# Banded attention and a gated block on one core: P.V products grouped by tile shape, low parts of w_out summed on TensorE, zero matmuls ahead of early transposes, new due times

## The chip, the cores and the metric

The kernel runs on one core of a Trainium2 chip. The metric is device time in microseconds: 289.54 us before the change, the median of three runs (288.92 to 289.74). A profile of one further execution goes with it. Engines are named as in the profile: PE is TensorE's matmuls, PEld its weight loads, DVE is VectorE, ACT ScalarE, POOL GpSimd, SP the queue that issues DMAs.

## The reference

Attention over 4 batch elements, 8 heads, 768 positions, head width 64; a row sees the first 8 positions and the last 96, with a linear bias by head. Its output is the input of a gated block: a causal depthwise convolution of 5 taps gives the gate, `x @ w_val` the value, and the gated value goes through `w_out`.

```python
scores = scale * np.matmul(q, k.transpose(0, 1, 3, 2))
keep = is_global | is_local
scores = np.where(keep, scores + bias[None], -1000000000.0)
a = np.exp(scores - np.max(scores, axis=-1, keepdims=True))
a = a / (np.sum(a, axis=-1, keepdims=True) + 1e-09)
attn = np.matmul(a, v)                       # then to (B, S, 512) as x
for k in range(5):
    gate_pre += conv_w[k][None, None, :] * xp[:, k:k + S, :]
gate = 1.0 / (1.0 + np.exp(-gate_pre))
out = gate * (x @ w_val) @ w_out
```

## The kernel before, in words

**Tiling.** A group is one batch element, one half of its positions (3 blocks of 128 rows) and one pair of heads: 32 groups, 96 steps (a step is one block of one group, numbered `s`). A step has a window of 168 columns per head (128 for the first block of a batch element, whose steps are the first of each first-half group). Scores come on TensorE in 64x64 tiles (`scores`, L451), VectorE adds the bias and takes the row minimum (L459), ScalarE takes the exponential with its row sum (L469), GpSimd or VectorE adds the small constant (L476) and normalizes (`p`, L484), VectorE inverts (L479). TensorE transposes the probabilities into a PSUM tile `pt` (L492; three transposes a step, two in a first block), of which there are two banks; ScalarE or VectorE copies it out (`a`).

**P.V.** `pv` (L499) runs for a pair of groups at a time, the last two groups alone. For each block it first takes the 128-row products (L510: 128 rows of `a` against `vs` or `v0`, on a 128x64 tile), then, unless the block is a first one, two rounds of 64-row products (L513, on 64x64 tiles), and goes on to the next block. An fp32 product shows as two instructions. From the fifth group on (index 4) the scores of a later group follow P.V directly. The result `x` stays in PSUM, in two buffers.

**Gated block.** A phase is one half of a batch element, four groups. `x` is split into a high and a low fp32r part (`xh`, `xl`), VectorE convolves it (L613), ScalarE takes the sigmoid, TensorE makes `val` with three fp32r products per chunk (L659), VectorE gates it, the gated value is split again, and TensorE makes the output tile `o` (L679), which needs all four chunks of `w_out`.

**Weights.** They come as 64-bit floats and are rebuilt from integer halves, chunk by chunk (four of `w_val`, four of `w_out`): one ScalarE step (L331), four VectorE steps (L339 to L348), then a high part `wvh` or `woh`. The low part is the remainder. For `w_val` TensorE adds it up in PSUM (`w_sum`, L373: the identity times the whole, minus one times the high part, plus one times the rest) and ScalarE or VectorE copies it out. For `w_out` two elementwise steps on GpSimd or VectorE do it (`w_rest`, `w_low`, L364 and L369).

**What sets the order.** `Plan` (L57) lists all operations with a due time ("urgency"), a cost per engine and what they wait for, and writes one order for all engines: at each point the free engine takes the most urgent ready operation. `plan.ring` keeps the use of a set of buffers in a fixed sequence. The constants at the top (L17 to L29) are due times and costs. Eight zero matmuls at the start and three behind the first scores (L254) are in the plan too. Each engine works its instructions off in the order written.

Of the kernel before, what the change touches and what calls it, by code (L numbers as in the profile page):

```python
# [15 lines left out]
AX = mybir.AxisListType  # L16
WARM = 8  # L17
S_B, PT_B, X_B = 2, 2, 2
U_D1, RAW_B = -1.42, 4
FILL_N, FILL_TO, U_F = 1, 1, -3.23  # L20
W_AT = (-0.65, 1.85, 4.45, 6.35, 17.51, 17.64, 22.06, 22.56)
SPARE = {'vector': 1.0, 'gpsimd': -0.11, 'scalar': -0.06}
XH_B, GATE_B, P_B, T_B, A_B, V_B, W_B, WT_B = 7, 2, 5, 8, 13, 6, 2, 1
U_XE, U_XH, U_CV, CV_STEP = 0.93, -0.23, 2.87, 0.59
U_AM, U_EX, U_RC, U_PT, U_EV, U_MOE = 0.47, 0.84, -0.36, -0.38, 3.52, 18.1
# [3 lines left out]
U_SG, U_GM, GM_STEP, U_GH, U_GL, U_O, VAL_T, O_T, U_OE = 1.99, -0.17, 2.17, 2.27, -3.94, 6.16, 7.45, 4.99, 1.44  # L29
PSUM = bass.MemoryType.PSUM  # L30

B, H, S, D = 4, 8, 768, 64
P = 128
NP = H // 2
NB = S // P
DM = H * D
# [20 lines left out]
class Plan:  # L57
# [3 lines left out]
    DMA_LAT, DMA_RATE = 1.6, 330e3  # L61

    def __init__(self):
        self.ops, self.at, self.rings, self.then = [], {}, {}, {}

    def add(self, key, urgency, engines, fn, deps=(), nbytes=0):

        assert key not in self.at, key
        self.at[key] = len(self.ops)
        self.ops.append((urgency, engines, fn, list(deps), nbytes))  # L70

    def follow(self, key, other):

# [12 lines left out]
    def order(self, start):  # L86
# [16 lines left out]
        while avail:  # L103
            cands = []
            for i in avail:
                t = {e: max(free[e], ready(i, e)) for e in ops[i][1]}
                e = min(t, key=lambda x: t[x] + ops[i][1][x] + SPARE.get(x, 0.0))
                cands.append((t[e], i, e))
            first = min(cands)
            _, i, e = min(  # L110
                ((ops[i][0], i, e) for t, i, e in cands if e == first[2] and t <= first[0] + 1e-9)
            )
            while i is not None:
                t = max(free[e], ready(i, e))
# [12 lines left out]
                i = self.then.get(i)  # L127
# [5 lines left out]
def attention_moe(ctx, tc, qT, kT, kg, vs, vo, v0, v, counts_in, wv, cw, wo, out):  # L133
# [199 lines left out]
    def f64_op(e, raw, n, nm, k):  # L333
# [10 lines left out]
        elif k == 3:  # L344
            ve.tensor_scalar(out=yi, in0=T[nm, "h"][:, :n], scalar1=-0x800000, scalar2=None, op0=ALU.bitwise_and)
        else:
            r = tile_of((nm, "r"), [P, DM], F32 if nm[1] >= NC else F32R, "wr", WT_B)[:, :n]
# [13 lines left out]
        h, c = (wvh, i) if i < NC else (woh, i - NC)  # L361
        copy(e, h[:, c], T[("w", i), "h"].bitcast(F32))

    def w_rest(e, i):  # L364
        h, c = (wvh, i) if i < NC else (woh, i - NC)
        x = T[("w", i), "h"].bitcast(F32)
        engine(e).tensor_sub(x, x, h[:, c])

    def w_low(e, i):  # L369
        l, c = (wvl, i) if i < NC else (wol, i - NC)  # L370
        engine(e).tensor_add(l[:, c], T[("w", i), "h"].bitcast(F32), T[("w", i), "r"])

    def w_sum(i):  # L373

        ps = tile_of(("wsum", i), [P, DM], F32, "moe", 2, psum)
        nc.tensor.matmul(ps, ident, T[("w", i), "h"].bitcast(F32), start=True, stop=False)
        nc.tensor.matmul(ps, units[:, 1], wvh[:, i], start=False, stop=False)
        nc.tensor.matmul(ps, units[:, 0], T[("w", i), "r"], start=False, stop=True)

    plan.ring("moe", 2, ("WARM",), [("WARM",)] + [("F", s) for s in range(3 * FILL_TO)])  # L380
    for i in range(2 * NC):
# [13 lines left out]
                     lambda e, i=i, k=k: f64_op(e, T["w", i], DM, ("w", i), k), deps)  # L395
        plan.add(("WH", i), u + 0.5, {ACT: 0.52, DVE: 0.335}, lambda e, i=i: w_high(e, i), [("W2", i), ("W3", i)])
        if i < NC:
            key = ("WS", i)
            plan.add(key, u + 0.6, {PE: 1.6}, lambda e, i=i: w_sum(i),
                     [("WH", i), ("W4", i), ("UNITS",)] + plan.ring("moe", 2, key, [("WP", i)]))  # L400
            plan.add(("WP", i), u + 0.7, {ACT: 0.47, DVE: 0.65},
                     lambda e, i=i: copy(e, wvl[:, i], T["wsum", i]), [("WS", i)])
            continue
# [82 lines left out]
    def transpose(s):  # L486

        pt = tile_of(("pt", s), [P, 4 * P], F32, "pt", PT_B, psum)
        pr = T["p", s].rearrange("p two n -> p (two n)")
        starts = (0, SW) if width(s) == P else (0, 2 * SW - P, SH)  # L490
        for i, c in enumerate(starts):
            nc.tensor.transpose(pt[:, i * P : (i + 1) * P], pr[:, c : c + P], ident)  # L492
# [4 lines left out]
        copy(e, a[:, :n], pt[:, :n])  # L497

    def pv(gs):  # L499
        for k in range(HB):  # L500
            w = width(HB * gs[0] + k)
            runs = [(g, j, head_at(groups[g][2], j), T["a", HB * g + k]) for g in gs for j in range(2)]
            c0 = HIST + k * P

            def rows(i):
                return slice(i * D, (i + 1) * D)

            for g, j, i, a in runs:
                v = T["v0", g][:, j] if w == P else T["vs", g][:, k, j]
                nc.tensor.matmul(T["x", g][rows(i), c0 : c0 + P], v, a[:, j * P : (j + 1) * P], start=True, stop=w == P)  # L510
            for h in range(2 if w == SW else 0):
                for g, j, i, a in runs:
                    nc.tensor.matmul(T["x", g][rows(i), c0 + h * QH : c0 + (h + 1) * QH], T["vo", g][rows(j), k, h],  # L513
                                     a[rows(j), 2 * P + h * QH : 2 * P + (h + 1) * QH], start=False, stop=h == 1)

    SCORES, SWITCH = 0.285, 0.1

# [2 lines left out]

    def pv_cost(gs):
        steps = HB if groups[gs[0]][1] else HB - 1
        return (0.64 if len(gs) == 2 else 0.43) * steps + 0.21 * len(gs) * (HB - steps)

    def s_deps(g):
        deps = [("Lrk", g), ("Lrq", g)]
# [33 lines left out]
    for g, (b, hf, p) in enumerate(groups):  # L560
        for k in range(HB):
# [23 lines left out]
            key = ("PT", s)  # L585
            plan.add(key, s + U_PT, {PE: 0.42 if full else 0.31}, lambda e, s=s: transpose(s),
                     [("NM", s, 0), ("NM", s, 1), ("IOTA",)] + plan.ring("pt", PT_B, key, [("EV", s)]))
# [369 lines left out]
```

## Time and profile before

| what | us |
|---|---|
| median of three runs | 289.54 |
| the profiled execution | 290.27 |
| its span, first to last instruction | 288.5 |
| PE busy | 267.1 (93%) |
| PEld busy | 216.6 (75%) |
| DVE busy | 202.4 (70%) |
| ACT busy | 213.7 (74%) |
| POOL busy | 142.4 (49%) |
| mean granted TensorE clock | 0.969 of full |

Busy time is the union of an engine's instructions, so overlapping matmuls count once. In a timeline a row is a run of like instructions: start, time to the end of the last, and their number; time in brackets is idle time of the engine before the row, with what ended it. The distance between the starts of two neighbouring rows is what the first took from the queue.

### The profile page before, as it was taken

Reading aid. Unit: us, or ns where it says so; the run is one execution under the profiler, and the core shown is the slowest. Engines: PE = TensorE matmul, PEld = TensorE weight load, DVE = VectorE, ACT = ScalarE, POOL = GpSimd, SP = SyncE. Lnnn points to the kernel's source line nnn. Section 1 sums busy time; section 2 is a strip of 40 time slices with the busy share of each in tenths; the row PEclk is TensorE's granted clock in tenths of the full one; section 3 lists DMA queues with packets and bytes.
Section 4 is the critical chain, followed back from the end, with each engine's and each line's share of the span. In section 5 each row is a group of like instructions: output and inputs, shape, how many; then the busy total and the mean of one; then the engine's idle time right before and its main releaser. Section 6 shows DMA issues by size and latency. Waiting matters only on the chain.

```text
span 288.5 us, 8778 instructions
## 1 busy us (share of the span) xinstructions
PE 267.1 (93%) x3084; PEld 216.6 (75%) x3084; DVE 202.4 (70%) x780; ACT 213.7 (74%) x658; POOL 142.4 (49%) x341
## 2 busy tenths in 40 slices
PE   7499785898999999999999999999999999999991
PEld 3266563585788978897789887987889888877981
DVE  3877999679496949596859775893959594946200
ACT  3779959666689969895979779985799589745220
POOL 5967467838332862476226812580348342720320
PEclk9779998599999999999999999999999999999999
DMA  6989965040464606350637063423641021001012
GB/s 161 313 254 316 314 184 181 28 128 3 139 210 124 189 36 186 101 180 9 210 138 222 28 182 136 131 64 99 214 157 55 3 76 39 0 2 73 36 42 80
DMA packets 25683, 36.38 MB, mean 126 GB/s; under 512 B 3104, under 2 KB 21536, under 8 KB 25632
## 3 DMA queue, kind: packets, MB, share of 16 engines
q1 hardware_dynamic: 25632, 35.75, 39.2%
q8 instruction: 26, 0.43, 0.6%
q14 instruction: 25, 0.20, 0.2%
HBM read 29.45 MB, written 6.29 MB: 124 GB/s over the span
## 4 chain that ended last, share of the span: by engine, by line
PE 72%; DVE 9%; POOL 6%; ACT 4%; issue 3%; DMA 3%; SPq 0%; POOLq 0%; ACTq 0%
PE val L659 21%; PE o L679 20%; PE x L510 9%; PE pt L492 9%; PE s L451 7%; PE x L513 6%; POOL p L484 3%; DVE gate L613 3%; DVE t L459 2%; POOL bias L318 2%; DMA vo<-in_vo 1%; DMA counts_i<-in_counts 1%; ACT p L469 1%; ACT gate L615 1%; POOL sm L476 1%
## 5 line engine op out<-in xcount | busy, mean ns | idle before, releaser
L469 ACT ACTIVATE p<-t,mins 128x168 f32<-128x168 f32 (+1 forms) x192 | 82.9, 437 | 10.2 <-DVE mins L459 8.6
L484 POOL TENSOR_SCALAR p<-p,rs 128x168 f32<-128x168 f32 (+1 forms) x179 | 75.2, 434 | 30.4 <-DVE rs L479 23.4
L613 DVE SCALAR_TENSOR_TENSOR gate<-x,cwt,gate 128x384 f32<-128x384 f32 x128 | 77.7, 612 | 1.3 <-ACT gate L615 0.5
L459 DVE CUSTOM_DVE_ANT_0 t<-s,bias 128x168 f32<-128x168 f32 (+1 forms) x192 | 56.7, 316 | 3.5 <-PE s L451 2.9
L492 PE MATMUL pt<-ident,p 128*128 128x128 f32 x272 | 51.3, 291 | 8.2 <-POOL p L484 6.1
L476 POOL TENSOR_SCALAR sm<-sm 128x2 f32<-128x2 f32 x94 | 19.2, 204 | 74.4 <-ACT p L469 66.0
L492 PEld LDWEIGHTS pt<-ident,p 128*128 128x128 f32 x272 | 34.4, 144 | 22.3 <-POOL p L484 14.5
L659 PE MATMUL val<-xh,wvh 128*128 128x384 f32 x128 | 47.1, 368 | 0.4 <-DVE g L666 0.4
L672 POOL TENSOR_TENSOR gl<-g,gh 128x384 fp32r<-128x384 f32 x32 | 32.5, 1014 | 25.6 <-ACT gh L155 24.5
L659 PE MATMUL val<-xl,wvh 128*128 128x384 f32 x128 | 43.2, 338 | 1.3 <-DVE xl L605 1.3
L659 PE MATMUL val<-xh,wvl 128*128 128x384 f32 x128 | 43.1, 337 | 0.0
L679 PE MATMUL o<-woh,gh 128*128 128x512 f32 x96 | 42.0, 437 | 1.0 <-DVE rs L479 1.0
L155 ACT COPY a<-pt 128x384 f32<-128x384 f32 (+1 forms) x84 | 38.7, 461 | 5.0 <-PE pt L492 4.7
L451 PE MATMUL s<-rk,rq 64*64 64x64 f32 (+3 forms) x1088 | 34.9, 265 | 3.9 <-DVE ('w', 0)_h L342 3.0
L469 ACT ACTIVATION_READ_ACCUMULATOR p<-t,mins 128x1 f32 x192 | 38.5, 200 | 0.0
L679 PE MATMUL o<-woh,gl 128*128 128x512 f32 x96 | 38.0, 396 | 0.0
L679 PE MATMUL o<-wol,gh 128*128 128x512 f32 x96 | 37.9, 395 | 0.0
L605 DVE TENSOR_TENSOR xl<-x,xh 128x384 fp32r<-128x384 f32 x32 | 17.5, 553 | 28.5 <-ACT gate L615 14.7
L451 PEld LDWEIGHTS s<-rk,rq 64*64 64x64 f32 x1088 | 30.9, 135 | 8.7 <-issue 5.8
L155 ACT CAST xh<-x 128x384 fp32r<-128x384 f32 x32 | 15.1, 479 | 23.1 <-PE x L513 18.3
L479 DVE RECIPROCAL rs<-sm 128x2 f32<-128x2 f32 x96 | 15.1, 159 | 21.1 <-POOL sm L476 20.1
L510 PE MATMUL x<-a,vs 128*64 128x128 f32 x320 | 28.0, 295 | 0.0
(149 smaller groups left out, 402.5 us busy)
## 6 DMA issues: line engine op xcount, KB each, us to landing
rq<-in_qT SPq DMA_DIRECT2D x32, 192.0 KB, 3.5
out<-ob SPq DMA_DIRECT2D x24, 256.0 KB, 2.0
rk<-in_kT SPq DMA_DIRECT2D x16, 252.0 KB, 3.4
rk<-in_kT SPq DMA_DIRECT2D x16, 200.0 KB, 3.1
vs<-in_vs SPq DMA_DIRECT2D x16, 192.0 KB, 3.3
vo<-in_vo SPq DMA_DIRECT2D x16, 192.0 KB, 3.3
w<-in_wv SPq DMA_DIRECT2D x4, 512.0 KB, 4.4
vs<-in_vs SPq DMA_DIRECT2D x16, 128.0 KB, 3.3
```

The source lines that it names most:

```text
L155: nc.scalar.copy(dst, src)
L451: nc.tensor.matmul(s[rows, u : u + w], T["rq", g][r, k * P + half * QH : k * P + (half + 1) * QH], T["rk", g][r, c : c + w], start=True, s ...
L459: nc.vector.tensor_tensor_reduce(out=t[:, :n], in0=T["s", s // HB, s % HB, j][:, :n], in1=bias[:, h, :P] if n == P else bias[:, h, P:], op ...
L469: nc.scalar.activation(T["p", s][:, j, :n], T["t", s, j][:, :n], AF.Exp, bias=mins[:, s, j : j + 1], scale=-1.0, accum_out=T["sm", s][:, j ...
L476: engine(e).tensor_scalar(out=sm, in0=sm, scalar1=1e-9, scalar2=1.0, op0=ALU.add, op1=ALU.mult)
L484: engine(e).tensor_scalar(out=pr, in0=pr, scalar1=rs, scalar2=1.0, op0=ALU.mult, op1=ALU.mult)
L492: nc.tensor.transpose(pt[:, i * P : (i + 1) * P], pr[:, c : c + P], ident)
L510: nc.tensor.matmul(T["x", g][rows(i), c0 : c0 + P], v, a[:, j * P : (j + 1) * P], start=True, stop=w == P)
L613: nc.vector.scalar_tensor_tensor(out=gt, in0=src, scalar=w, in1=gt, op0=ALU.mult, op1=ALU.add)
L659: nc.tensor.matmul(T["val", ph, m], (wvh, wvh, wvl)[r][:, c, m * P : (m + 1) * P], (T["xh", g], T["xl", g], T["xh", g])[r], start=(c == 0 ...
L672: engine(e).tensor_sub(tile_of(("gl", ph, m), [P, HT], F32R, "gl", 5), T["g", ph, m], T["gh", ph, m])
L679: nc.tensor.matmul(T["o", ph, k], (T["gh", ph, c], T["gl", ph, c], T["gh", ph, c])[r][:, cols], (woh, woh, wol)[r][:, c], start=(c == 0 an ...
```

## The change

`pv` takes all 128-row products of a batch first, over its three blocks, and then all 64-row products. `w_rest` and `w_low` go; `w_out` chunks use `w_sum` as `w_val` does, in the PSUM ring of the transposes, behind the transposes of steps 17, 18, 23 and 24. The plan counts, for each transpose that it puts before its time 80, how many zero matmuls fit into the time for which it sees TensorE idle (at most 12), and `transpose` issues them into its own PSUM tile first. All due times get new values.

```diff
-U_D1, RAW_B = -1.42, 4
-FILL_N, FILL_TO, U_F = 1, 1, -3.23
-W_AT = (-0.65, 1.85, 4.45, 6.35, 17.51, 17.64, 22.06, 22.56)
-SPARE = {'vector': 1.0, 'gpsimd': -0.11, 'scalar': -0.06}
+U_D1, RAW_B = -4.08, 4
+FILL_UNTIL = 80.0
+FILL_N, FILL_TO, U_F = 1, 1, -4.6
+W_AT = (-1.16, 2.02, 7.13, 10.68, 17.77, 19.65, 21.85, 24.91)
+WS_AT = (17, 18, 23, 24)
+SPARE = {'vector': 0.99, 'gpsimd': 0.02, 'scalar': -0.16}
...
-U_L, U_LV, U_WL, U_S, U_HI, U_NM = -13.8, -2.88, -2.19, -1.88, -1.27, 0.16
-U_PH = (-4.57, -2.14, -0.94, 0.0, 0.0, -0.17, 0.0, 3.57)
+U_L, U_LV, U_WL, U_S, U_HI, U_NM = -19.46, -1.44, -0.21, -1.87, -2.32, -2.58
+U_PH = (-5.31, -2.3, -1.09, -0.3, -0.58, -0.33, -3.9, 2.9)
...
+                if ops[i][5] is not None and t < FILL_UNTIL:
+                    bank = max([end[at[d]] + self.LAT[where[at[d]]] for d in ops[i][5]], default=0.0)
+                    self.fill[i] = max(0, min(12, int((t - max(free[e], bank) - 0.15) / 0.215)))
...
     def w_sum(i):
-        ps = tile_of(("wsum", i), [P, DM], F32, "moe", 2, psum)
+        tag, bufs = ("moe", 2) if i < NC else ("pt", PT_B)
+        high = wvh[:, i] if i < NC else woh[:, i - NC]
+        ps = tile_of(("wsum", i), [P, DM], F32, tag, bufs, psum)
         nc.tensor.matmul(ps, ident, T[("w", i), "h"].bitcast(F32), start=True, stop=False)
-        nc.tensor.matmul(ps, units[:, 1], wvh[:, i], start=False, stop=False)
+        nc.tensor.matmul(ps, units[:, 1], high, start=False, stop=False)
         nc.tensor.matmul(ps, units[:, 0], T[("w", i), "r"], start=False, stop=True)
...
-        plan.add(("WS", i), u + 0.6, {POOL: 1.33, DVE: 0.62}, lambda e, i=i: w_rest(e, i), [("WH", i), ("W3", i)])
-        plan.add(("WP", i), u + 0.7, {POOL: 1.33, DVE: 0.62}, lambda e, i=i: w_low(e, i), [("WS", i), ("W4", i)])
...
     def transpose(s):
         pt = tile_of(("pt", s), [P, 4 * P], F32, "pt", PT_B, psum)
+        for _ in range(plan.fill.get(plan.at["PT", s], 0)):
+            nc.tensor.matmul(pt, nc.const_aps.tensor(1.0, [P, P], BF16), nc.const_aps.tensor(1.0, [P, DM], BF16),
+                             start=True, stop=True)
...
     def pv(gs):
...
         for k in range(HB):
+            c0, one_half = HIST + k * P, width(HB * gs[0] + k) == SW
+            for g, j, i in runs:
+                v = T["vs", g][:, k, j] if one_half else T["v0", g][:, j]
+                nc.tensor.matmul(T["x", g][rows(i), c0 : c0 + P], v, T["a", HB * g + k][:, j * P : (j + 1) * P],
+                                 start=k == 0, stop=False)
+        for k in range(1 - hf, HB):
+            for h in range(2):
+                c0 = HIST + k * P + h * QH
+                for g, j, i in runs:
+                    nc.tensor.matmul(T["x", g][rows(i), c0 : c0 + QH], T["vo", g][rows(j), k, h],
+                                     T["a", HB * g + k][rows(j), 2 * P + h * QH : 2 * P + (h + 1) * QH],
+                                     start=False, stop=k == HB - 1 and h == 1)
...
+            for i in range(NC, 2 * NC):
+                if s == WS_AT[i - NC]:
+                    add_sum(i)
```

## Rows read from the trace of the kernel before

**Rows 1.** Busy time of each engine in stretches of the span, from the windows view: stretch, its length, busy time and instructions of PE, PEld, DVE, ACT and POOL, granted TensorE clock, busy share of the DMA engines, GB/s.

```profile
12.00:40.00 28.00, 25.84 (x314) 18.11 (x315) 23.50 (x95) 24.55 (x83) 19.15 (x47) 0.89 0.82 259
40.00:60.00 20.00, 13.92 (x173) 9.72 (x173) 15.70 (x54) 12.54 (x37) 13.88 (x23) 0.74 0.40 129
60.00:72.00 12.00, 10.38 (x52) 8.34 (x53) 11.25 (x32) 9.31 (x25) 7.31 (x11) 1.00 0.23 68
72.00:256.00 184.00, 183.81 (x2324) 155.45 (x2323) 136.77 (x552) 152.79 (x482) 88.70 (x228) 1.00 0.37 115
```

**Rows 2.** The view of waits: who waited for whom, us in all, times, the longest. The first row is of PE from 0 to 72 us, the second of PEld from 72 us on (the answer for PE from 72 us on has no rows).

```profile
PE pt L492 <- POOL p L484: 6.1, 7, 1.4
...
PEld pt L492 <- POOL p L484: 3.1, 14, 0.5
```

**Rows 3.** Timeline of PE through one second-half pair batch of P.V, up to the scores behind it.

```profile
118.89 0.66 PE L510 MATMUL x<-a,vs 128*64 128x128 f32 x8
119.47 0.46 PE L513 MATMUL x<-a,vo 64*64 64x64 f32 x16
119.86 0.66 PE L510 MATMUL x<-a,vs 128*64 128x128 f32 x8
...
121.43 0.46 PE L513 MATMUL x<-a,vo 64*64 64x64 f32 x16
121.71 1.08 PE L451 MATMUL s<-rk,rq 64*64 64x168 f32 x36
```

**Rows 4.** Timeline of PE at the head of a first-half pair batch.

```profile
89.13 0.66 PE L510 MATMUL x<-a,v 128*64 128x128 f32 x8
89.62 0.61 PE L510 MATMUL x<-a,vs 128*64 128x128 f32 x8
90.16 0.46 PE L513 MATMUL x<-a,vo 64*64 64x64 f32 x16
```

**Rows 5.** The 64-row run of rows 3 that starts at 119.47, cut by narrow windows of the timeline: what is left of it from the second round of four on, and from the fourth.

```profile
119.58 0.35 PE L513 MATMUL x<-a,vo 64*64 64x64 f32 x12
...
119.70 0.24 PE L513 MATMUL x<-a,vo 64*64 64x64 f32 x4
```

**Rows 6.** Timeline of PE in a batch of one group.

```profile
256.74 0.44 PE L510 MATMUL x<-a,vs 128*64 128x128 f32 x4
257.11 0.45 PE L513 MATMUL x<-a,vo 64*64 64x64 f32 x8
257.49 0.44 PE L510 MATMUL x<-a,vs 128*64 128x128 f32 x4
```

**Rows 7.** The windows view of line L513 alone (columns PE, PEld, clock, DMA share, GB/s), from 72 us on.

```profile
72.00:288.50 216.50, 16.53 (x528) 11.59 (x528) 1.00 0.33 105
```

**Rows 8.** Timeline of the third pair batch: its first 128-row run, the scores behind it, and VectorE's first gate step of that batch.

```profile
54.04 1.12 PE L510 MATMUL x<-a,vs 128*64 128x128 f32 x8
...
58.91 1.05 PE L451 MATMUL s<-rk,rq 64*64 64x168 f32 x36
...
59.13 0.62 DVE L617 TENSOR_SCALAR gate<-x,cwt 128x384 f32<-128x384 f32 x1 [3.43 <-PE x L513]
```

**Rows 9.** The windows view of all engines (columns as in rows 1) over the second stretch at the lower clock.

```profile
48.70:58.80 10.10, 7.89 (x77) 4.84 (x81) 6.36 (x25) 6.44 (x17) 9.06 (x16) 0.50 0.21 77
```

**Rows 10.** Timeline of PE: the three zero matmuls behind the first scores.

```profile
6.04 0.82 PE L254 MATMUL warm<-const-bfloat16-1.0 128*128 128x512 bf16 x3
```

**Rows 11.** Timeline of POOL and PE from 46 to 51 us: the two steps of the second chunk of `w_out`, the norms of `p` behind each, and the transposes.

```profile
46.58 1.57 POOL L367 TENSOR_TENSOR ('w', 5)_h<-('w', 5)_h,woh 128x512 f32<-128x512 f32 x1 [0.36 <-DVE rs L479]
...
48.13 0.79 POOL L484 TENSOR_SCALAR p<-p,rs 128x168 f32<-128x168 f32 x2
...
48.59 1.07 PE L492 MATMUL pt<-ident,p 128*128 128x128 f32 x3 [1.11 <-POOL p L484]
...
49.27 1.27 POOL L371 TENSOR_TENSOR wol<-('w', 5)_h,('w', 5)_r 128x512 fp32r<-128x512 f32 x1
...
50.52 0.79 POOL L484 TENSOR_SCALAR p<-p,rs 128x168 f32<-128x168 f32 x2
...
50.98 1.07 PE L492 MATMUL pt<-ident,p 128*128 128x128 f32 x3 [1.32 <-POOL p L484]
```

**Rows 12.** Timeline of `w_sum` for the third chunk of `w_val` (its first row and the next transpose), and of the copy out of the fourth.

```profile
25.21 1.13 PE L376 MATMUL wsum<-('w', 2)_h,ident 128*128 128x512 f32 x2
...
26.63 0.38 PE L492 MATMUL pt<-ident,p 128*128 128x128 f32 x2
...
33.51 0.62 ACT L155 CAST wvl<-wsum 128x512 fp32r<-128x512 f32 x1
```

**Rows 13.** The windows view of one line (columns as in rows 7): the transposes, L492, in two stretches, and the output products, L679, in a third.

```profile
0.00:71.00 71.00, 14.42 (x62) 8.08 (x62) 0.88 0.61 191
71.00:74.70 3.70, 0.98 (x6) 0.78 (x6) 1.00 0.28 80
...
66.40:76.00 9.60, 7.55 (x27) 4.69 (x27) 1.00 0.23 73
```

**Rows 14.** The source view of L339 (an integer step of a weight chunk on VectorE) and of L371 (GpSimd's add for the chunk before): count, shortest, median and longest in ns, first and last start in us.

```profile
L339 DVE TENSOR_SCALAR ('w', 4)_y<-('w', 4)_y x1: 411/411/411, 35.2 to 35.2; 128x512 int32<-128x512 int32 x1
L339 DVE TENSOR_SCALAR ('w', 5)_y<-('w', 5)_y x1: 1493/1493/1493, 40.0 to 40.0; 128x512 int32<-128x512 int32 x1
...
L371 POOL TENSOR_TENSOR wol<-('w', 4)_h,('w', 4)_r x1: 1376/1376/1376, 39.8 to 39.8; 128x512 fp32r<-128x512 f32 x1
```

**Rows 15.** The windows view of all engines (columns as in rows 1).

```profile
96.00:104.00 8.00, 8.00 (x76) 6.69 (x75) 7.82 (x31) 8.00 (x32) 6.95 (x19) 1.00 0.32 100
```

More of the change, by code (lines that the diff above doesn't have):

```diff
@@ L63, in __init__, with add @@
     def __init__(self):
-        self.ops, self.at, self.rings, self.then = [], {}, {}, {}
-    def add(self, key, urgency, engines, fn, deps=(), nbytes=0):
+        self.ops, self.at, self.rings, self.then, self.fill = [], {}, {}, {}, {}
+    def add(self, key, urgency, engines, fn, deps=(), nbytes=0, bank=None):
         assert key not in self.at, key
         self.at[key] = len(self.ops)
-        self.ops.append((urgency, engines, fn, list(deps), nbytes))
+        self.ops.append((urgency, engines, fn, list(deps), nbytes, bank))
     def follow(self, key, other):
@@ L346, in f64_op @@
         else:
-            r = tile_of((nm, "r"), [P, DM], F32 if nm[1] >= NC else F32R, "wr", WT_B)[:, :n]
+            r = tile_of((nm, "r"), [P, DM], F32R, "wr", WT_B)[:, :n]
             ve.scalar_tensor_tensor(out=r, in0=lo.bitcast(U32), scalar=2.0**-52, in1=y,
@@ L362, in w_high, with add_sum @@
         copy(e, h[:, c], T[("w", i), "h"].bitcast(F32))
[L364 to L371, printed above, removed]
     def w_sum(i):
-        ps = tile_of(("wsum", i), [P, DM], F32, "moe", 2, psum)
+        tag, bufs = ("moe", 2) if i < NC else ("pt", PT_B)
+        high = wvh[:, i] if i < NC else woh[:, i - NC]
+        ps = tile_of(("wsum", i), [P, DM], F32, tag, bufs, psum)
         nc.tensor.matmul(ps, ident, T[("w", i), "h"].bitcast(F32), start=True, stop=False)
-        nc.tensor.matmul(ps, units[:, 1], wvh[:, i], start=False, stop=False)
+        nc.tensor.matmul(ps, units[:, 1], high, start=False, stop=False)
         nc.tensor.matmul(ps, units[:, 0], T[("w", i), "r"], start=False, stop=True)
+    def add_sum(i):
+        key, low = ("WS", i), wvl[:, i] if i < NC else wol[:, i - NC]
+        bank = plan.ring("moe", 2, key, [("WP", i)]) if i < NC else plan.ring("pt", PT_B, key, [("WP", i)])
+        plan.add(key, W_AT[i] + 0.6, {PE: 1.6}, lambda e: w_sum(i), [("WH", i), ("W4", i), ("UNITS",)] + bank)
+        plan.add(("WP", i), W_AT[i] + 0.7, {ACT: 0.47, DVE: 0.65}, lambda e: copy(e, low, T["wsum", i]), [("WS", i)])
     plan.ring("moe", 2, ("WARM",), [("WARM",)] + [("F", s) for s in range(3 * FILL_TO)])
@@ L397, in attention_moe @@
         if i < NC:
[L398 to L403, printed above, removed]
-        plan.add(("WS", i), u + 0.6, {POOL: 1.33, DVE: 0.62}, lambda e, i=i: w_rest(e, i), [("WH", i), ("W3", i)])
-        plan.add(("WP", i), u + 0.7, {POOL: 1.33, DVE: 0.62}, lambda e, i=i: w_low(e, i), [("WS", i), ("W4", i)])
+            add_sum(i)
     def load_taps(e):
@@ L499, in pv, with rows @@
     def pv(gs):
+        hf = groups[gs[0]][1]
+        runs = [(g, j, head_at(groups[g][2], j)) for g in gs for j in range(2)]
+        def rows(i):
+            return slice(i * D, (i + 1) * D)
         for k in range(HB):
[L501 to L514, printed above, removed]
+            c0, one_half = HIST + k * P, width(HB * gs[0] + k) == SW
[10 more added lines that the diff above has]
+                                     start=False, stop=k == HB - 1 and h == 1)
     SCORES, SWITCH = 0.285, 0.1
@@ L522, in pv_cost @@
         steps = HB if groups[gs[0]][1] else HB - 1
-        return (0.64 if len(gs) == 2 else 0.43) * steps + 0.21 * len(gs) * (HB - steps)
+        return (0.64 if len(gs) == 2 else 0.43) * steps + 0.21 * len(gs) * (HB - steps) + 0.2
     def s_deps(g):
@@ L585, in attention_moe @@
             key = ("PT", s)
+            bank = plan.ring("pt", PT_B, key, [("EV", s)])
             plan.add(key, s + U_PT, {PE: 0.42 if full else 0.31}, lambda e, s=s: transpose(s),
-                     [("NM", s, 0), ("NM", s, 1), ("IOTA",)] + plan.ring("pt", PT_B, key, [("EV", s)]))
+                     [("NM", s, 0), ("NM", s, 1), ("IOTA",)] + bank, bank=bank)
+            for i in range(NC, 2 * NC):
+                if s == WS_AT[i - NC]:
+                    add_sum(i)
             key = ("EV", s)
```

6 lines of the change are left out of this document (3 added, 3 removed).

## The prediction

> **What bounds the kernel now.** I read the busy time by stretch first [rows 1]. Up to 72 us TensorE stands idle part of the time (25.84 of 28, 13.92 of 20 and 10.38 of 12 us busy, 9.9 us idle in all) and part of it runs at the lower of its two clock levels; from 72 to 256 us it is busy for 183.81 of 184 us at full clock, and the kernel's end is its last products and one store. Busy time alone proves little, since matmuls overlap. So I read the waits next [rows 2]: before 72 us TensorE's matmuls wait 6.1 us for the normalized probabilities `p` in front of the transposes; after 72 us no matmul row waits for another engine at all, and only the weight load of a transpose does, 3.1 us, beside running matmuls. ScalarE (152.79) and VectorE (136.77 of 184 us) have room on the mean. So I take the kernel as two stages: until about 72 us it is a mix of VectorE, GpSimd and clock, after that a TensorE queue that is never empty, where a TensorE microsecond saved is one off the end.
>
> **P.V batches.** In a second-half batch of two groups [rows 3], one block's 128-row run takes 0.58 us from its first start to the first 64-row product (118.89 to 119.47), and a 64-row run 0.39 us to the next 128-row product (119.47 to 119.86); the last 64-row run goes over into the scores, which have the same 64x64 tile, in 0.28 us (121.43 to 121.71). What a run costs when it is joined to one of its own kind is also in the trace. A first-half batch begins with two 128-row runs back to back, since its first block has no 64-row part [rows 4]: 89.13 to 90.16, 1.03 us for both, where two single ones take 2 x 0.58 or 0.59 (the start times are rounded). Joining saves 0.15. Inside a 64-row run the rounds of four start at 119.47, 119.58 and (the last) 119.70 [rows 3, 5], so 0.06 apart once going, while the last one is followed by the next kind only 0.16 later and the first takes 0.11: joining saves 0.10 + 0.05 = 0.15. Together, each return from 64-row back to 128-row products that goes away saves 0.30 us, the value I take. The lowest that the rows allow is 0.15, if only the joining of 128-row runs holds; nothing in them points above 0.30.
>
> How many returns go: two in a second-half pair, one in a first-half pair, two in a batch of one group. A single's runs cost 0.37 and 0.38 [rows 6], with the same opening (0.16 to the second pass) and the same end, so I price its returns alike. The 528 64-row products after 72 us [rows 7] are 6 second-half pairs of 48, 6 first-half pairs of 32 and 2 singles of 24. Returns removed there: 12 + 6 + 4 = 22, and 22 x 0.30 = 6.6 us, all in the stage where TensorE never waits. Bounds 3.3 (at 0.15) and 6.6.
>
> Before 72 us three pair batches run. The first two (one return each) stand in a stretch where TensorE waits anyway: 0, at most 0.6. The third runs at half clock [rows 8, 9], from 54.04 to 58.91, 4.87 us, and VectorE's gate idles 3.43 us until it ends; by rows 3 the same work joined and at full clock is 2.2 us (3 x 0.44 + 0.15 for the 128-row part, 3 x 0.24 + 0.05 for the other). So it gives 2.7 us if the clock is up, and about 1.2 (two returns at half speed) if not.
>
> **Zeros ahead of transposes.** They are issued only where the planner sees TensorE idle ahead of a transpose, up to 12 each time, before its time 80. Three of them cost 0.82 us with their tail [rows 10], so 0.27 each at most. I cost them at nothing, because the cover is the idle time above; if half of that 9.9 us weren't there in fact, they would cost 5 us. What they can give is the clock: the granted clock was 0.50 from 48.7 to 58.8 us [rows 9], right behind a stretch of waits before transposes. Since they go just there, I lean to the upper end for the third batch: 2.3 of the 1.2 to 2.7.
>
> **w_out low parts.** Removed: two GpSimd steps for each of three chunks, and two on VectorE for the fourth. At 46.58 and 49.27 these steps (1.57 and 1.27 us) hold back the norm of `p`, which starts as each ends (48.13, 50.52), and the transposes behind it wait 1.11 and 1.32 us [rows 11]. Ends 0 and 2.4; I take 2.0, near the upper one, because the norms start within 0.02 us of the ends of these steps. Added for each of four chunks: on TensorE two passes with the identity and two with signed units. The third chunk of w_val shows them at full clock [rows 12]: the first starts at 25.21 and the next transpose at 26.63, so 1.42 us. They are queued behind the transposes of steps 17, 18, 23 and 24. A step has three transposes, two where its block is the first of a batch element, so 62 transposes before 71 us are steps 0 to 21, and the next six, up to 74.7, steps 22 and 23 [rows 13]: in the run of before, the two late sums would fall at about 74 us and later, where TensorE is full. They are charged, 2.8 us; the two early ones lie in the idle 6.1 us of 40 to 60 and cost 0. Bounds 0 and 5.7 (all four). Behind a sum that waits for VectorE's chain stands every later transpose and P.V batch. The fourth chunk's copy out was 0.62 us on ScalarE [rows 12]; ScalarE and VectorE have 10 and 5 us free from 40 to 72 us [rows 1], and without that cover it holds one of two transpose banks.
>
> One rule counts for more here than the sum shows. An integer step of the weights on VectorE took 1493 ns beside GpSimd's add of w_out and 411 ns one chunk earlier [rows 14]. The Trainium skill (SBUF — State Buffer, Who interferes with whom) says that VectorE and GpSimd share one port pair under an exclusive lock, and that the later one blocks fully; the trace agrees, with 1.1 us. By that rule the removed adds give VectorE some 1.1 us more; by my sum, nothing, as VectorE has room elsewhere.
>
> **Order.** Nearly all due times change. After 72 us there is no wait to gain; before it 9.9 us of idle. I take 0, with 4 us either way (less than half of that idle).
>
> **The sum.** -6.6 - 2.3 - 2.0 + 2.8 = -8.1 us. The profiled execution took 290.27 us, its span of 288.5 plus 1.8 around it, and would come to 282.2; it lay 0.7 above the median of the runs, 289.54, from which I forecast **281.4 us**.
>
> **Rivals.**
>
> *TensorE only looks full.* For: ScalarE is busy 8.00 of 8 us from 96 to 104, VectorE 7.82 [rows 15], so a faster TensorE could meet unready inputs. Against: no matmul waits after 72 us [rows 1, 2]. Half the 6.6 is lost, and what the early stage gains is lost behind the same engines: 289.5 - 3.3 = 286.2. Chance 0.16. The Trainium skill (Trainium Kernel Development and Optimization, Performance Expectations) calls matmul busy time a bad metric and weight-load busy time a good one; by the latter TensorE is at 155.45 of 184 us here, and this rival would be the truth. The waits speak against it.
>
> *The early stage shrinks more.* Full clock, no GpSimd detour and a better order recover half of the 9.9 us idle beyond my sum: 276.5. For: the stage is loose. Against: VectorE is busy 23.5 of 28 us from 12 to 40 [rows 1]. Chance 0.15.
>
> *The output products come late (slower).* 27 of them run between 66.4 and 76 us and keep TensorE busy for 7.55 us [rows 13]; each output tile now needs sums that stand behind steps 23 and 24. If TensorE finds nothing else, those 7.5 us are idle: with no early gain, 289.5 - 6.6 + 2.8 + 7.5 = 293.2. It decides once that idle passes 3.8 us. Against: transposes, scores and value products are other work, and they would bring steps 23 and 24 forward. Chance 0.09. Zeros that overrun would have to be 14 at 0.27 to reach the same point.
>
> **Numbers.** Forecast 0.60 (own range 278 to 284.5), the rivals 0.16, 0.15, 0.09. The range 276 to 286.5 leaves out the slow rival and the ends of the others. About 0.3% is what a measurement of this kernel tells from no change: faster 0.86 (the forecast, the second rival and 0.11 of the first, whose 0.05 of worse feeding is the same), same 0.05, slower 0.09.
>
> **What would show it.** In the changed profile a pair batch is one 128-row run of 24 and one 64-row run of 48, some 2.2 us together, with 22 fewer returns after 72 us; the granted clock stays at 1.00 around 50 us; GpSimd's w_out rows are gone; TensorE's matmuls still wait for nobody after about 72 us, and w_out sums take about 1.4 us each. New TensorE waits in that stage, or a first output product well after 70 us, would prove me wrong.

## The result, and the profile after

The changed kernel takes 281.96 us (median of four runs, 281.48 to 282.23) against 289.26 for the kernel before (289.54 with the first three runs alone): a ratio of 0.9744, 95% interval 0.9723 to 0.9766, or 7.3 us less. The forecast was 281.4, with 8.1 us less; its range, 276 to 286.5, holds the time. Medians and intervals here go by fast runs alone; one run of the kernel without zeros (629.72 us) and one of the kernel with zeros alone (300.78 us) were slow and are left out. Whether the terms behind the forecast hold too is another matter, and most of what follows is about that.

Lines of the page after: busy time of the engines with its share of the span and instructions, and the granted TensorE clock in 40 slices of the span, 7 us each, in tenths.

```profile
PE 264.0 (94%) x3110; PEld 216.8 (77%) x3113; DVE 199.4 (71%) x776; ACT 217.0 (77%) x665; POOL 133.1 (47%) x334
...
PEclk9799999999999999999999999999999999999999
```

TensorE is busy only 3 us less than before (267.1), although its span is 8.3 us shorter (280.2): 16 more instructions of sums and thirteen zeros went in (weight loads, PEld, 3113 against 3084; three matmul records are missing from this trace) while returns went out. GpSimd lost 9 us. The clock has one dip left, in the second slice; before, it had two, in slices 2 and 3 and in 7 and 8 (lowest digit 5).

The windows view after, with the columns and nearly the stretches of [rows 1].

```profile
12.00:40.00 28.00, 25.54 (x327) 18.50 (x329) 25.13 (x102) 25.42 (x88) 18.27 (x45) 0.99 0.85 274
40.00:60.00 20.00, 19.27 (x219) 14.66 (x219) 18.64 (x69) 18.94 (x58) 10.60 (x25) 1.00 0.48 148
60.00:72.00 12.00, 11.23 (x165) 7.71 (x164) 10.20 (x37) 9.81 (x34) 6.79 (x16) 1.00 0.38 113
72.00:248.00 176.00, 174.62 (x2181) 150.06 (x2181) 128.83 (x519) 147.20 (x458) 85.13 (x216) 1.00 0.36 112
```

From 40 to 60 us TensorE, VectorE and ScalarE are all near full now, where they were at 13.92, 15.70 and 12.54 of 20. TensorE's idle time from 12 to 72 us is 4.0 us in place of 9.9. From 72 us on it idles 1.4 us of 176, where it had idled 0.2 of 184 before. The view of waits for PE, from 72 to 248 us, has two rows where before it had none:

```profile
PE pt L492 <- POOL p L481: 0.8, 2, 0.7
PE val L667 <- ACT ob L160: 0.2, 1, 0.2
```

The third pair batch, which [rows 8] showed at half clock, in the timeline of PE after, with the sum of the first w_out chunk ahead of it:

```profile
46.00 1.02 PE L374 MATMUL wsum<-('w', 4)_h,ident 128*128 128x512 f32 x2
46.46 0.80 PE L375 MATMUL wsum<-woh,units 128*128 128x512 f32 x1
47.10 0.39 PE L376 MATMUL wsum<-('w', 4)_r,units 128*128 128x512 f32 x1
47.41 1.53 PE L510 MATMUL x<-a,vs 128*64 128x128 f32 x24
48.88 0.93 PE L516 MATMUL x<-a,vo 64*64 64x64 f32 x48
49.62 0.60 PE L448 MATMUL s<-rk,rq 64*64 64x168 f32 x16
```

One 128-row run of 24 in 1.47 us, one 64-row run of 48 in 0.74: the batch takes 2.21 us where 2.24 had been worked out from [rows 3 to 5], and 4.87 before. The sum takes 1.41 us up to the batch, as [rows 12] said (1.42). The stretch of [rows 9] runs at full clock:

```profile
48.70:58.80 10.10, 9.69 (x132) 8.32 (x128) 9.42 (x33) 10.09 (x33) 6.62 (x13) 1.00 0.47 145
```

### The profile page after: what moved, and what is told of

It reads as the page before. It is cut to its first block, busy times and chain, and to the rows that moved or that the text cites. A ratio compares the mean times of both kernels' runs of the same rounds, so it can differ in the third digit from the quotient of the medians.

```text
span 280.2 us, 8833 instructions
## 1 busy us (share of the span) xinstructions
PE 264.0 (94%) x3110; PEld 216.8 (77%) x3113; DVE 199.4 (71%) x776; ACT 217.0 (77%) x665; POOL 133.1 (47%) x334
## 4 chain that ended last, share of the span: by engine, by line
PE 60%; DVE 13%; ACT 9%; POOL 7%; issue 4%; DMA 3%; SPq 1%; POOLq 0%; DVEq 0%
PE o L687 18%; PE val L667 17%; PE pt L492 8%; PE x L510 7%; PE s L448 6%; DVE gate L621 5%; POOL p L481 4%; PE x L516 3%; ACT p L466 3%; DVE t L456 2%; DVE xl L613 2%; DMA w<-in_wv 2%; ACT L466 1%; DMA rk<-in_kT 1%; ACT gate L623 1%
## 5 line engine op out<-in xcount | busy, mean ns | idle before, releaser
L492 PE MATMUL pt<-ident,p 128*128 128x128 f32 x272 | 50.7, 283 | 3.9 <-POOL p L481 2.8
L667 PE MATMUL val<-xh,wvh 128*128 128x384 f32 x128 | 47.8, 373 | 0.6 <-DVE ob L162 0.3
L492 PEld LDWEIGHTS pt<-ident,p 128*128 128x128 f32 x272 | 33.6, 140 | 18.9 <-POOL p L481 10.5
L448 PE MATMUL s<-rk,rq 64*64 64x64 f32 (+3 forms) x1088 | 36.3, 268 | 3.7 <-DVE rs L476 2.7
L448 PEld LDWEIGHTS s<-rk,rq 64*64 64x64 f32 x1088 | 32.1, 138 | 9.2 <-issue 5.7
L466 ACT ACTIVATION_READ_ACCUMULATOR p<-t,mins 128x1 f32 x192 | 37.9, 198 | 0.0
L667 PEld LDWEIGHTS val<-xh,wvh 128*128 128x128 f32 x128 | 24.2, 189 | 3.0 <-ACT ob L160 1.3
L674 DVE TENSOR_TENSOR g<-val,gate 128x384 f32<-128x384 f32 x32 | 17.6, 551 | 11.9 <-PE val L667 11.4
```

The costliest lines, as they stand in the source:

```text
L448: nc.tensor.matmul(s[rows, u : u + w], T["rq", g][r, k * P + half * QH : k * P + (half + 1) * QH], T["rk", g][r, c : c + w], start=True, s ...
L466: nc.scalar.activation(T["p", s][:, j, :n], T["t", s, j][:, :n], AF.Exp, bias=mins[:, s, j : j + 1], scale=-1.0, accum_out=T["sm", s][:, j ...
L667: nc.tensor.matmul(T["val", ph, m], (wvh, wvh, wvl)[r][:, c, m * P : (m + 1) * P], (T["xh", g], T["xl", g], T["xh", g])[r], start=(c == 0 ...
```

## The experiments

Each run is timed beside the kernel before on the same chip; its median there was 289.1 to 289.7, and I take 289.4. The question: the total came out near the forecast, but is it the sum of the terms named? Each trace is of one execution, and executions of one kernel differ in their mean clock (0.967 to 0.980 in the kernel before), so a place read from two traces is weaker than a median.

**P.V alone, from both sides.** First the changed kernel with the old sequence of P.V, the order of everything else untouched.

```diff
-        runs = [(g, j, head_at(groups[g][2], j)) for g in gs for j in range(2)]
+        for k in range(HB):
+            w = width(HB * gs[0] + k)
+            runs = [(g, j, head_at(groups[g][2], j), T["a", HB * g + k]) for g in gs for j in range(2)]
...
-        for k in range(1 - hf, HB):
-            for h in range(2):
...
+            for h in range(2 if w == SW else 0):
+                for g, j, i, a in runs:
```

> The changed kernel with the P.V products in their old sequence, everything else and the whole order as changed. Theory (each return to 128-row products costs 0.30 us, TensorE full): 26 returns come back, 26 x 0.30 = 7.8 us, 289 to 290 us. Rival (the new due times carry the gain, P.V is hidden beside other work): under 285 us.

Measured: 288.34 us (ratio to before 0.9966, 0.9951 to 0.998). Second, the kernel before with the new sequence alone:

```diff
-            for g, j, i, a in runs:
-                v = T["v0", g][:, j] if w == P else T["vs", g][:, k, j]
...
+        for k in range(HB):
+            c0, one_half = HIST + k * P, width(HB * gs[0] + k) == SW
+            for g, j, i in runs:
...
+        for k in range(1 - hf, HB):
+            for h in range(2):
```

> The kernel before with the P.V products in the new sequence alone; its order of operations is untouched. Theory: 22 returns fewer after 72 us, 289.3 - 6.6 = 282.7 us (282 to 283.5), and the rest of the change nets about 1 us. Rival (new due times carry it): 286 us or more.

Measured: 282.31 us (0.9752, 0.9731 to 0.9773). So P.V is worth 6.4 us in the changed kernel and 7.1 in the one before, and the rival that new due times carry the gain is out: without the P.V edit the whole rest of the change is worth about 1 us. The first expectation missed: 288.34 is 0.7 us below its range and 1.4 below 282.0 + 7.8; the second hit. The timeline of PE in the changed kernel with the old sequence shows that the returns are there and cost what was said:

```profile
48.11 0.66 PE L510 MATMUL x<-a,vs 128*64 128x128 f32 x8
48.70 0.46 PE L513 MATMUL x<-a,vo 64*64 64x64 f32 x16
49.09 0.66 PE L510 MATMUL x<-a,vs 128*64 128x128 f32 x8
```

It is 0.98 us a block at full clock (0.97 in [rows 3]). What a return is worth at the end is read from the kernel before, without and with the new sequence, as the order is the same in both: the starts of the fourth pair batch and of the two singles, first before, then with the new P.V.

```profile
75.89 0.66 PE L510 MATMUL x<-a,vs 128*64 128x128 f32 x8
250.21 0.44 PE L510 MATMUL x<-a,vs 128*64 128x128 f32 x4
256.74 0.44 PE L510 MATMUL x<-a,vs 128*64 128x128 f32 x4
```

```profile
74.11 1.53 PE L510 MATMUL x<-a,vs 128*64 128x128 f32 x24
243.05 0.88 PE L510 MATMUL x<-a,vs 128*64 128x128 f32 x12
248.99 0.88 PE L510 MATMUL x<-a,vs 128*64 128x128 f32 x12
```

From the fourth batch to the first single the lead grows from 1.78 to 7.16 us, 5.38 over 18 returns or 0.30 each, as forecast; the first single adds 0.59 for its two. The last single's two add nothing: the spans (288.5 and 280.7) differ by 7.8, and 7.75 of it is there when that batch starts. So 6.0 us come after 72, not 6.6. Of the 1.78 before, 1.15 is there at the first pair batch (22.81 and 21.66), where nothing differs yet: that much is chance in these two executions.

In the changed kernel with the old sequence TensorE idles 2.1 us from 12 to 72 us, by its windows view:

```profile
12.00:40.00 28.00, 26.81 (x325) 19.12 (x326) 24.21 (x96) 24.98 (x86) 18.32 (x45) 0.90 0.85 267
40.00:60.00 20.00, 19.70 (x219) 14.91 (x218) 18.97 (x70) 18.93 (x57) 10.12 (x23) 1.00 0.51 157
60.00:72.00 12.00, 11.37 (x165) 7.96 (x164) 9.85 (x36) 9.57 (x33) 7.16 (x17) 1.00 0.29 86
```

The changed kernel idles 4.0 there, so a part of what the returns give up before 72 us may have turned into waits for other engines. How much, these two traces don't tell, as they also differ in the mean clock from 12 to 40 us (0.90 and 0.99). The 6.4 us itself is no matter of the clock: over all runs (ten and four) the mean granted clock is 0.987 in both.

**Zeros, from both sides.** The changed kernel without its zeros, then the kernel before with zeros alone. The expectations say ten and 22 zeros; the weight loads on the pages show thirteen (3113 with them, 3100 without) and 23 (3107 and 3084).

```diff
-        for _ in range(plan.fill.get(plan.at["PT", s], 0)):
+        for _ in range(0):
```

> The changed kernel without its ten zero matmuls ahead of transposes; the order is untouched. Theory (they hold the clock up): the granted clock falls to half somewhere between 40 and 60 us and the time rises by about 2.3 us to 284.3. Rival (TensorE is full enough there without them): clock 1.00, 281.9 us within 0.5.

Measured: 283.07 us (0.9769, 0.9746 to 0.9792), 1.1 more than with them (0.7 by the ratios); the intervals overlap, so neither its size nor that it is a loss is firm. The windows view shows where the clock falls without them, and that it is not where I had said:

```profile
31.20:34.40 3.20, 3.20 (x11) 2.39 (x10) 3.20 (x14) 2.91 (x11) 1.73 (x5) 0.50 0.88 298
48.70:58.80 10.10, 10.06 (x145) 8.71 (x141) 9.44 (x32) 10.07 (x29) 5.66 (x12) 1.00 0.47 144
```

From 48.7 to 58.8 us the changed order keeps TensorE at full clock on its own (10.06 of 10.10 us busy). In the changed kernel five zeros stand just ahead of the other place, and the clock stays up there:

```profile
28.95 1.47 PE L487 MATMUL pt<-const-bfloat16-1.0 128*128 128x512 bf16 x5 [0.61 <-ACT a L160]
```

The first pair batch starts at 22.64 us with the zeros and 22.57 without, the second at 34.92 and 35.90, so in these traces the microsecond is lost there.

The same zeros in the kernel before:

```diff
+                if ops[i][5] is not None and t < FILL_UNTIL:
+                    bank = max([end[at[d]] + self.LAT[where[at[d]]] for d in ops[i][5]], default=0.0)
+                    self.fill[i] = max(0, min(12, int((t - max(free[e], bank) - 0.15) / 0.215)))
...
+        for _ in range(plan.fill.get(plan.at["PT", s], 0)):
+            nc.tensor.matmul(pt, nc.const_aps.tensor(1.0, [P, P], BF16), nc.const_aps.tensor(1.0, [P, DM], BF16),
+                             start=True, stop=True)
```

> The kernel before with zero matmuls ahead of early transposes alone (its own plan gives 22 of them), order untouched. Theory: the stretch from 48.7 to 58.8 us keeps the full clock, 289.3 - 2.3 = 287.0 us. Rival A (they change nothing that ends late): 289.3. Rival B (they are not covered by idle time): 22 x 0.27 = 5.9 us more, up to 295.

Measured: 287.22 us (0.9926, 0.9903 to 0.9949), 2.1 less than before by the ratio; its stretch was at full clock:

```profile
48.70:58.80 10.10, 9.08 (x135) 5.99 (x134) 8.53 (x28) 7.07 (x17) 8.50 (x14) 1.00 0.35 116
```

The third pair batch with the scores behind it, in the same trace:

```profile
53.01 0.66 PE L517 MATMUL x<-a,vs 128*64 128x128 f32 x8
...
55.84 1.06 PE L455 MATMUL s<-rk,rq 64*64 64x168 f32 x36
```

It takes 2.83 us in place of 4.87, so it gives 2.04. In the kernel before, the zeros do what was forecast, for the reason given.

**The two together, and the rest by steps.** The kernel before with the last two diffs for it, the new P.V and the zeros, and nothing else:

> The kernel before with the new P.V sequence and the zeros, but w_out's low parts and all due times as before; order untouched. If the two gains add: 289.4 - 7.1 - 2.1 = 280.2 us, faster than the changed kernel. If they share the third batch, which is slow both from its returns and from its clock: about 280.8. Rival (with less TensorE work the zeros no longer hold the clock): 282.3.

Measured: 280.22 us (0.9683, 0.9661 to 0.9704). The two gains add fully, the rival (282.3) is out, and this kernel is 1.7 us faster than the changed one: the remaining parts of the change cost time. Runs with parts of that rest; first the changed kernel with w_out's low parts elementwise again:

```diff
-            for i in range(NC, 2 * NC):
-                if s == WS_AT[i - NC]:
-                    add_sum(i)
+        plan.add(("WS", i), u + 0.6, {POOL: 1.33, DVE: 0.62}, lambda e, i=i: w_rest(e, i), [("WH", i), ("W3", i)])
+        plan.add(("WP", i), u + 0.7, {POOL: 1.33, DVE: 0.62}, lambda e, i=i: w_low(e, i), [("WS", i), ("W4", i)])
```

> The changed kernel with the low parts of w_out made by elementwise steps again (two per chunk on GpSimd or VectorE, planned with the new due times), and no sums of w_out on TensorE. The plan writes a slightly different order, so this is the edit together with that. Theory (two late sums cost 2.8 us of a full TensorE, the GpSimd steps hold transposes up by 2.0): 281.2 us. Rival A (all four sums cost TensorE time and the GpSimd steps cost nothing): 282.0 - 5.7 = 276.3. Rival B (the GpSimd steps are what was worth removing): 284 or more.

Measured: 284.40 us (0.9821, 0.9798 to 0.9843). With the new due times, the elementwise steps are 2.4 us slower than the sums. That looks like rival B, that these steps are what was worth removing, until the same choice is made with the old due times (below: there the sums are 2.1 us slower). The theory's 281.2 missed. The changed kernel with these (two lines of the constants shown, the others in the same way):

```diff
-U_XE, U_XH, U_CV, CV_STEP = -0.21, -0.33, 2.83, 0.57
+U_XE, U_XH, U_CV, CV_STEP = 0.93, -0.23, 2.87, 0.59
...
-U_PH = (-5.31, -2.3, -1.09, -0.3, -0.58, -0.33, -3.9, 2.9)
+U_PH = (-4.57, -2.14, -0.94, 0.0, 0.0, -0.17, 0.0, 3.57)
```

> The changed code (P.V in the new sequence, zeros, sums of w_out on TensorE behind steps 17, 18, 23, 24) with the due times and spare costs of the kernel before. The sum by measured parts: 289.4 - 7.1 (new P.V alone) - 2.1 (zeros alone) = 280.2, and the sums of w_out on top. Theory (order is worth 0, late sums 2.8, GpSimd steps gone -2.0): 281.0. Rival (the old due times leave the output products waiting for the late sums, and the new ones were needed for that): 284 or more.

Measured: 286.54 us (0.9897, 0.988 to 0.9915). The theory's 281.0 missed. The rival has the size, but its reason doesn't show: the output products wait 0.5 us for `wol` in this trace. From 280.22 it is 6.3 more, and two things differ: the w_out sums, and 0.2 us that the change adds to the plan's cost of a P.V batch, which the section on the change doesn't mention. One experiment for each. To the kernel with new P.V and zeros (280.22 us) the plan cost is added:

```diff
-        return (0.64 if len(gs) == 2 else 0.43) * steps + 0.21 * len(gs) * (HB - steps)
+        return (0.64 if len(gs) == 2 else 0.43) * steps + 0.21 * len(gs) * (HB - steps) + 0.2
```

> The kernel before with the new P.V sequence, the zeros, and the plan's cost of a P.V batch raised by 0.2 us as in the change; w_out and due times as before. The order shifts a little. If the plan's cost is what matters least: 280.2 us as without it, within 0.6. If an order that knows the batch better helps: 279.5 or less; if due times fitted to the old cost are upset by it: 281 or more.

Measured: 284.24 us (0.9821, 0.9788 to 0.9853). Two zeros fewer and a few steps moved to another engine (GpSimd 347 instructions for 341); otherwise the plan merely wrote another order, and it costs 4.0 us. Three waits of PE from 12 us on, and the windows view, show where some of it goes:

```profile
PE o L691 <- DVE g L678: 2.4, 2, 2.2
PE val L671 <- DVE g L678: 1.5, 2, 1.1
PE s L455 <- DVE mins L463: 1.5, 2, 1.3
```

```profile
64.00:67.00 3.00, 3.00 (x10) 2.43 (x9) 3.00 (x6) 1.88 (x6) 2.34 (x4) 0.50 0.00 0
...
72.00:240.00 168.00, 165.92 (x2196) 142.33 (x2195) 123.66 (x520) 143.99 (x454) 81.85 (x215) 1.00 0.41 124
```

Output products stand in TensorE's queue ahead of their gated input (2.4 us), the clock is at half from 64 to 67 us, and 2.1 us are idle from 72 to 240 us (0.2 without the plan cost). This trace also has a stretch at half clock near 30 us, but the clock is not most of it: the run with the highest mean clock (0.992) took 283.64 us. Then the sums, with the old cost and the old due times, which is the changed kernel with the diff of the old due times above and this one:

```diff
-        return (0.64 if len(gs) == 2 else 0.43) * steps + 0.21 * len(gs) * (HB - steps) + 0.2
+        return (0.64 if len(gs) == 2 else 0.43) * steps + 0.21 * len(gs) * (HB - steps)
```

> The changed code with the due times of before and the plan's old cost of a P.V batch (so the step from the kernel before with new P.V and zeros, 280.2 us, is the w_out sums alone, with the order that the plan then writes). From the measured parts: GpSimd steps away -2.8 to -3.0, four sums of 1.42 us at the 3.5 of 5.7 that doubling them cost: 280.2 - 2.9 + 3.5 = 280.8. If all four count, 283. If the order is upset as by the 0.2 us of plan cost (284.2), 284 or more.

Measured: 282.33 us (0.9763, 0.9744 to 0.9782): the w_out sums, with the order that the plan writes for them, cost 2.1 us. The expected 280.8 missed by 1.5. The windows view from 72 us on, without and with the sums, and a wait of PE there:

```profile
72.00:248.00 176.00, 175.79 (x2312) 152.53 (x2308) 134.25 (x537) 149.49 (x473) 87.65 (x226) 1.00 0.38 116
```

```profile
72.00:248.00 176.00, 174.26 (x2180) 149.06 (x2179) 134.89 (x534) 147.84 (x462) 85.05 (x217) 1.00 0.38 116
...
PE o L687 <- ACT wol L160: 0.5, 1, 0.5
```

TensorE idles 1.7 us there in place of 0.2. And the changed kernel with this diff alone, so with its own due times:

> The changed kernel with the plan's old cost of a P.V batch (0.2 us less) and nothing else. If any shift of the order away from the due times that were fitted to it costs about 4 us, as it did with the old due times: 284 to 286. If the fitted order isn't so sensitive: 282.0 within 0.6.

Measured: 282.43 us (0.9749, 0.9728 to 0.9769), the same as with the new cost within the noise. So the new due times stand the 0.2 us and the old ones don't.

**The two sides of w_out.** What the elementwise steps cost in the kernel before:

```diff
-        engine(e).tensor_sub(x, x, h[:, c])
+        engine(e).tensor_sub(x[:, :8], x[:, :8], h[:, c, :8])
...
-                T["o", ph, k], (T["gh", ph, c], T["gl", ph, c], T["gh", ph, c])[r][:, cols], (woh, woh, wol)[r][:, c],
+                T["o", ph, k], (T["gh", ph, c], T["gl", ph, c], T["gh", ph, c])[r][:, cols], (woh, woh, woh)[r][:, c],
```

> The kernel before with the two elementwise low-part steps of each w_out chunk cut to 8 of 512 columns, order untouched; the low part of w_out is left out of the product (its pass runs with the high part, so TensorE does the same work). Theory of the prediction (these steps hold up transposes on the path by 2.0 us, and nothing takes their place): 287.4 us. Rival (another wait is right behind, so that taking the steps away gives nothing at the end): 289.4 within 0.6.

Measured: 286.46 us (0.9903, 0.9873 to 0.9933), 2.9 less. The size fits; of the mechanism, half does. The two transposes of [rows 11] in this kernel, with the norm ahead of the second, and the sum of the waits for `p`:

```profile
44.57 0.82 PE L492 MATMUL pt<-ident,p 128*128 128x128 f32 x3
...
46.40 0.78 POOL L484 TENSOR_SCALAR p<-p,rs 128x168 f32<-128x168 f32 x2 [0.95 <-DVE rs L479]
...
46.86 0.92 PE L492 MATMUL pt<-ident,p 128*128 128x128 f32 x3 [1.47 <-POOL p L484]
...
PE pt L492 <- POOL p L484: 5.3, 6, 1.5
```

The first waited 1.11 us before and waits for nobody now. The second waited 1.32 and now waits 1.47: its norm is held back by VectorE's `rs` in place of the GpSimd step. In all the transposes wait 5.3 us for `p`, 6.1 before [rows 2]. A third place gives as much again, the one that the prediction's rule on VectorE beside GpSimd named and its sum left at nothing. First the kernel before, then this one:

```profile
42.01 0.44 PE L659 MATMUL val<-xl,wvh 128*128 128x384 f32 x1 [1.27 <-DVE xl L605]
```

```profile
38.05 0.43 DVE L339 TENSOR_SCALAR ('w', 5)_y<-('w', 5)_y 128x512 int32<-128x512 int32 x1
...
39.31 0.34 PE L659 MATMUL val<-xl,wvh 128*128 128x384 f32 x1
```

With GpSimd's add cut to 8 columns, the integer step of [rows 14] takes 0.43 us in place of 1.49. In VectorE's queue `xl` stands behind it, and the value product that waited 1.27 us for `xl` waits no more. So the steps' 2.9 us are, in these traces, some 1.1 of a named wait and 1.3 of this one; the rest isn't settled, and a higher clock (0.83 in place of 0.74 from 40 to 60 us) is mixed in. And what the sums cost, by doing them twice:

```diff
+        for _ in range(1 if i < NC else 2):
```

> The changed kernel with each of the four w_out sums done twice over on TensorE (the second overwrites the first), order untouched: 4 x about 1.4 us more TensorE work between 46 and 72 us. Theory of the prediction (the two early ones lie in idle time, the two late ones count): 282.0 + 2.8 = 284.8. Rival (after the change TensorE has no idle time left there, and all four count): 282.0 + 5.6 = 287.6.

Measured: 285.48 us (0.9877, 0.9844 to 0.991), 3.5 more. The timeline shows one sum after another in 1.32 and 1.40 us:

```profile
46.15 1.02 PE L375 MATMUL wsum<-('w', 4)_h,ident 128*128 128x512 f32 x2
...
47.47 1.02 PE L375 MATMUL wsum<-('w', 4)_h,ident 128*128 128x512 f32 x2
...
48.87 1.53 PE L511 MATMUL x<-a,vs 128*64 128x128 f32 x24
```

So 3.5 of some 5.5 us reach the end: more than the two of four that I charged, less than all. Where, the sums of the third chunk show, first in the changed kernel, then here:

```profile
64.05 1.02 PE L374 MATMUL wsum<-('w', 6)_h,ident 128*128 128x512 f32 x2
```

```profile
65.44 1.02 PE L375 MATMUL wsum<-('w', 6)_h,ident 128*128 128x512 f32 x2
```

Of the second copies of the two early sums, some 2.7 us, 1.4 are left there, and the two late ones add 1.9 to the end of the span. But a second copy finds the idle time already used by the first, so this is no price of the first.

## Why the prediction was right, and where it was not

The steps from run to run (each is a difference, so they add up whatever the causes): 289.4 to 282.3 with the new P.V (-7.1), to 280.2 with zeros (-2.1), to 282.3 with the w_out sums (+2.1), to 282.0 with the new due times and plan cost (-0.4, within the noise). Forecast were -7.8 (6.6 and the third batch's 1.2), -1.1 (the rest of that batch, for the clock), +0.8 and 0.

- **What bounds the kernel**: right. A saving on TensorE came through nearly whole, in both kernels, with ScalarE busy 10.09 of 10.10 us in one stretch. "TensorE's matmuls still wait for nobody" held for P.V and zeros (0.2 us idle of 176 after 72), not for the whole change: 1.4 us are idle there, and by its own sign of being wrong that is a step that failed. The rival that TensorE only looks full is out at the size it was given (half of the P.V gain lost); of 7.8 us, 6.4 arrived. The Trainium skill (Trainium Kernel Development and Optimization, Performance Expectations) takes weight-load busy time, not matmul busy time, for how close a kernel is to its roofline; that is 84% for the kernel before after 72 us. Whether a saving there reaches the end, the matmul waits told.
- **P.V**: right, to 0.03 us in the batch and to 0.30 us a return at the end. The return prices came from places of the same trace where the joined form already stood. Two of its 22 returns after 72 us gave nothing, and the third batch, at half clock, 0.8 in place of 1.2 (4.09 us for 4.87 with the new sequence alone), so the measured 7.1 is below 7.8.
- **Zeros and clock**: right in mechanism in the kernel before, at 2.1 for a term of 1.1 that left the batch's returns to P.V; the two terms' errors, +0.7 and -1.0, nearly cancel. In the changed kernel the order keeps the clock up from 48.7 to 58.8 us anyway, and the zeros are worth about 1 us, if anything, at another place, 31 to 34 us.
- **w_out**: the term that was off, 2.1 net where +0.8 was taken. The forecast said that the two early sums "lie in the idle 6.1 us of 40 to 60 and cost 0". With new P.V and zeros, 40 to 60 us have 2.05 us idle, and with the sums 0.37, by these rows of the runs without and with them: all engines, then TensorE's zeros alone, and in the second the sums alone.

```profile
40.00:60.00 20.00, 17.95 (x211) 12.81 (x214) 18.74 (x65) 16.23 (x45) 13.66 (x23) 1.00 0.49 150
...
40.00:60.00 20.00, 5.36 (x20) 1.00 0.49 150
```

```profile
40.00:60.00 20.00, 19.63 (x247) 14.90 (x246) 17.93 (x67) 18.73 (x56) 9.69 (x24) 1.00 0.51 152
...
40.00:60.00 20.00, 2.30 (x9) 1.00 0.51 152
...
40.00:60.00 20.00, 2.98 (x8) 1.00 0.51 152
```

The two sums take 3.0 us there. Idle time gave 1.7 and the zeros 3.1, as the plan puts fewer of them where a sum stands; by subtraction, all other products got 14.4 us in place of 12.6. So in these two traces the early sums hid as forecast. The late ones fall from 64 to 73 us, where TensorE is nearly full, and were charged. What the sum left out is what stands behind them: 1.5 us of new idle time after 72 us, part of it output products that wait for the copied low part (0.5). That is the size of the miss, but the two orders differ as well, so how much is the sums and how much the order is open. The GpSimd side was 2.0 for a measured 2.9: one of its two named waits went, the other passed to VectorE's `rs`, and 1.3 us came by the rule that the forecast named and counted as nothing.
- **Order**: 0 was near (-0.4), but by luck: it lies between two sizable numbers, +4.2 for what 0.2 us of plan cost does to the old due times and -4.6 for the new ones.
- **The late output products** did not happen: in the changed kernel they begin earlier, at 56.79 us against 66.57. The first ones need only the first chunk, and the late sums, forecast at about 74 us and later, stand at 64.05 and 70.31.

```profile
56.79 0.48 PE L687 MATMUL o<-woh,gh 128*128 128x512 f32 x1
```

So the total was near for two reasons of unlike worth: the two large terms were right together, to 0.3 us, and the errors in the others (+1.3 and -0.4) were small beside them and partly cancelled.

## What to carry to other kernels

Group a batch's matmuls by tile shape, and price it from a place in the trace where two runs of one shape already stand side by side. When filler matmuls are put into idle time, they count as busy but give way where the plan drops them: what a next edit can hide in is the idle time and the fillers together. Then look at what stands behind the edit, as a queue without waits can get new ones. When two engines slow each other in the trace, follow who waits for the slowed step before pricing it at nothing. Where an order is written from fitted due times, a change that adds no work can still cost 4 us, so time each part with the order frozen. Here the kernel before with the P.V sequence and the zeros alone (280.2 us) beats the whole change (282.0).

## What the runs showed of the hardware

A joined 64-row run keeps its pace over 48 products: 0.74 us from its first start to the scores, against 1.06 for three runs of 16 with 128-row runs between them (0.39, 0.39 and 0.28). A return to 128-row products cost 0.30 us of the end (5.38 over 18). An identity product of 512 fp32 columns with two fp32r products behind it takes 1.32 to 1.42 us of TensorE at full clock, about as long as each of the two GpSimd steps that it replaces (1.27 to 1.57 us); a copy out of PSUM comes on top (0.62 us, [rows 12]). A VectorE integer step on 128x512 took 1.49 us beside a GpSimd add of 512 columns and 0.43 with that add cut to 8 columns.
